# Retention followed by two MLPs: attention from chunk 4 on in half chunks of 64 tokens

## The chip, the cores and the metric

The kernel runs on one core of a Trainium2 chip. The metric is the device time of one execution in microseconds (us); smaller is better. The kernel before takes 568.31 us (median of 3 runs, 567.98 to 568.66).

## The reference

The inputs are q, k and v of shape (2 batches, 8 heads, 768 tokens, 64 features). The result of the attention, laid out as 1536 tokens by 512 features, goes through two MLPs (512 to 2048 to 512).

```python
for t in range(S):                     # retention, per batch and head
    state = gamma * state + outer(k[t], v[t])
    y[t] = scale * (q[t] @ state)
h = x @ w_in                           # first MLP
P = a0 + a1*h + a2*h**2 + a3*h**3
Q = 1 + |b0|*|h| + |b1|*h**2
x = (P / (Q + 1e-6)) @ w_out
h = x @ w_in2                          # second MLP
out = (h * sigmoid(h)) @ w_out2
```

## The kernel before, in words

The attention works in 12 chunks of 128 tokens (`attention(c, ...)`, chunk c is block c // 2 of batch c % 2). Decay factors are folded into v, into the mask and into the output, so that a chunk is plain matmuls. Each chunk has three groups of fp32 matmuls on TensorE:

- **SC** (`sc`, line 503): scores. 8 calls (4 head pairs, 2 heads), each 64 features deep, 128 weight columns, 128 moving columns, into two PSUM banks. VectorE multiplies each bank by the causal mask (`am`, line 510; 128x512, twice a chunk).
- **OUTS** (`outs`): line 545, masked scores times v, 8 calls 128 deep with 64 weight columns and 128 moving columns; and from chunk 2 on line 558, the state times q, 8 calls 64 deep, 64 by 128. For the latter GpSimd copies half of q to the other partition half (`qm`, line 492). VectorE then scales the result (`xf`, two of 128x256), ScalarE rounds it to the high part `xh`, and GpSimd or VectorE takes the low part `xl`.
- **GROW** (`grow`, line 529): k times v for the state, 8 calls 128 deep, 64 by 64; not for chunks 10 and 11. VectorE (ScalarE for chunks 0 and 1) adds the bank to the state `bd`. GROW needs v scaled by the decays (`vn`, line 498, on GpSimd; VectorE for chunk 0).

In the trace each fp32 matmul call is two matmul records, each with its own weight load: 16 records for 8 calls.

The MLPs are matmuls of 128x128 weights by 512 moving columns in three products of split operands: `mm_in` at line 595 (12 a step), `mm_out` at line 672 (3 for each of 4 output banks a step). Weights come by DMA as 64-bit words and are taken apart by ScalarE, VectorE and GpSimd (`weights`, `parted`); `il`, `ol` and `gl` are low parts made on GpSimd in the first part of the kernel. From line 839 on (`joint`) and `remaining` the second MLP follows. The last output bank leaves in two halves (`ends`), the three before it by ScalarE (line 705).

The order of all 2344 operations is written out in a table (`ORDER`, unpacked in `Flow.order`); each engine executes its own operations in that order. Around the change the table of before has, on TensorE: chunk 4's SC, steps 0 and 1 of the first MLP, then in one run OUTS of chunk 4, SC of 5 and 6, GROW of 4, OUTS and GROW of 5, GROW and OUTS of 6. For chunks 7 to 9 SC stands alone between MLP matmuls, and OUTS with GROW behind it stand together; for 10 and 11 SC and OUTS each stand alone. A stretch of attention matmuls with MLP matmuls on both sides is called an island below.

PSUM has eight banks: a0, a1, acc0 to acc3, h0, h1. SC and OUTS of chunk 4 and of chunks 6 to 11 use a0 and a1; the state grows in h0, or acc2 and acc3 for chunks 4 to 6.

Of the kernel before, what the change touches and what calls it, by code (L numbers as in the profile page):

```python
# [11 lines left out]
F32 = mybir.dt.float32  # L12
# [11 lines left out]
R = {"xp": (3,), "vd": (0,), "early": ((0, 7), (2, 8), (3, 9), (4, 12)), "gqd": 0, 'lw': -463.92, 'T0': 689.59, 'tau0': 13.93, 'tau1': 122.19, 'c0': -129.63, 'dc': 67.51, 'conv': 39.61, 'half': 427.29, 'absl': -34.77, 'raw': 455.03, 'ret': 752.06, 'spl': -417.39, 'hi': 301.24, 'lo': 31.56, 'inn': -277.93, 'later': -32.81, 'split': -554.53, 'out': 359.39, 'evac': -363.13, 'qload': -20.08, 'scl': 238.79, 'sc': 858.37, 'am': -44.15, 'gr': 112.48, 'av': -547.62, 'bd': 198.47, 'xh': -201.14, 'xl': 110.32, 'glp': 48, 'lop1': 24, 'lop2': 30, 'scp': 4, 'ps': 17, 'ksc': 103.89, 'qa': -467.29, 'ka': 0, 'late': 20, 'mid': 4, 'pev': -317.29, 'pld': -385.01, 'cg': -489.85, 'wm': 6, 'mk': 26.43, 'ck': 21.3, 'g2': (1, 0, 2), 'ch0': 269.21, 'ch1': -102.81, 'ch2': 64.3, 'ch3': 22.33, 'ch4': -52.46, 'ch5': 5.42, 'ch6': -78.23, 'ch7': 237.84, 'ch8': 90.06, 'ch9': -61.88, 'ch10': -106.39, 'ch11': -212.52, 'ru0': 218.22, 'lu0': -107.8, 'ru1': 40.68, 'lu1': -106.06, 'ru2': 91.09, 'lu2': 146.01, 'ru3': -37.17, 'lu3': -39.51, 'rhalf': 125.38, 'wsum': 20.0, 'kd': 4, 'hb': 20, 'turned': ()}  # L24
# [12 lines left out]
    '|3L%12|4f)Jcf9f9pAzTxCHSr7v{uU@E)GP2iOA%@hK$0eE1GtLNELXpCA$5fZUiLKf@Pz0ex@)Cc{Qp00C3rWw;24eX$_+#zHs<pF??k2FY<KHp',
    '9YL1RLT=D2l~!AVx*Pez*_&;~GqfEieu?$AA@(u`w3Mz1R|4;WsGQ8rNb8tb`S@DVD@Mm;}GaD)<!+#vxc4t70{*j!9AR2W*3-a3q$)VVD}z;Bfp',
    'AYhW4NfIs18T!%HW7UsovSQ|&-blixEaSV>d(YOga<2W3TGjI!jM>BCN*1-cf0Vm=loP}kv39iS#@NaC3?Qt7!$2ph^=i+RvhdZ!4?ZnCWEuO|b*',
    'aeSbSNs~g;ePBxH}N3;iofAJoR16eXY4^esXO+-TUZ+F;%)4Rcd!!<qPy4uhtWb@g#X|R>_@-gJ-m;H@en@1DYzIP;=lMGzQiNgmtNsn6nc%l=y&',  # L40
    'W-Z}A-trtj$uF2QNI3Wv~lIDp>c2V9CDaUgxd;bb&|qL9)b_!;ZtBYcc!&?zd7q^Y=qA{33HQw;ioD=8txq^FpOmSbXCfwAZu0>!2$n1qtjDoRGD',
    'Fgc~55tx!vQEEckg@00J>P^pZ8D^oiw3*`2pGb5J<I*}xLs=;s1$vHKDLdt$EyPrmR$^MpNx3LDrK96`0k=^e`jLuJUfMy$DIX=E^pv0CQwb_SUr',
    '{L<N+oGMRilh_5jRk2dO|<ZF3Ln@s4T^!BJ=}QrwmkxYSL<2L*=MEt;QO(kv7q8tVOk{4(+67RFEoAU8+Y9=o#&%J=B6OVSW0V8c=g;NEPWJwWL>',
    '6nEs_I)QVcux73E((s}%k+EF8FPaWtfJ*QDLhThO<s!A{DGIpe~G>$6MUo@U3&`WwmA7~aep-wcL=F&u(M8DD}dQFpQFMUH@X+ABWIrK9%rS#z!$',
    '`~rq6naYwX%YQKjcGe&4V`H!?W1?}o(|A{>O%8qF+Ha9^fzS))94@_p(WIfj?xS|M29I;C>So#CAvs6=@?z6?BO__APkwqQo2IRDO<QoIl^@MNFj',
    'VC3Rmzd#tk_Ghh>x{<O(%{hLd!PEL@}O^gCU{>v)=8hZ__xBnUU@7D*@^iibksEX5Cr!U_CBx5-11kT^s_ln^x}4Cg3Gh!&EDJ5)44IEgnfceqD2',
    'L$Z)OqzENLiSQ4775<<z6g{+%7$I*c74B25Fd*a!vpHp`9qNQsAz#QJe&yeI9-rdU;VzX4-%8yugUg0;p<XB-+J_3EVwl4*Lx)g5bP69r>hN_K7#',
    'f6*p;%}b=JG+V6e@=T;WWn%T|%5ND8veB0&v&RIgAVAL!&SxbPL~wp`me@$xXs>P8$Y?`P@BJ3$r*~IKoxK#PEIiAq)${!-%ke7xD?N9wvo%e1<d',
    '2uc3MPHjE4tLYp9bh!68e{w<v39$|i{621u}Z9}WDCrl14!h-N~ILbZ4FX0%s3{69?usSpgU--w+I`j@xLc1_E{1oPey`g_t7}kcdVOm%d7KOfHd',
    'gvDxhYevyI2+c5C1GaR7}kfSVN=)_eh*{9=CD7E4(GxjVRkqW{tkV@mM|(T3kSojusm!Hhr+#ZAsi0d!o_et90`AgqhW5i6z+%ZA;QPP<?tX}2@k',  # L50
    '`6;oq<#Tn&%H$`FOGg~wrMh{ij@lW;vm=Q-hNSQT!B<KfTnESw0t!}D-6B;}}lE5zWK9E*2_WSpH}gcSTTB<GZzievN1keYLH9KIdWa2|dY;&Ki?',
    '9nx}MJ{8{coA6Kg#2+{pzYTXnI?m1S!)MMW@i-r!3F$dM-wiqCV~EcsIRk$R3Ag}f<j<iXXX0A?6_?^HQkt_$AuhvTLUt+3wVC-{sKehfat>)Hg}',
    'EFP*X1Hyp6hcxR!+zj_-k&(iMb*-;6xm_H7DUp+>m>58#b=YZ5gBySK)Sy(wH-IZ*I?7xGLw7_R^O-NH%W5eK;$3;1b-Q`|*$L+>r-xSNVoJ@j!0',
    'MMY*H=#5H*kcjitqiq}dt9?aiK7cS1-WGolsAm8&M?#iQ?C9e$OZaj{w^J2~?HFyj!<&8X)yUTd)AwTdE-XatD56&eMxh4P3xn&uj<xM<^H}i7d!',
    'YySouizHEjn8p&ZY5iJB{$>N(p&!G?))>a;-1`7e&GweoqO<~+*!WkUUHsC@@l@s!?}y>;LCiGNAON=BWw5`U*TQ6PTI<D7P-$4_$oi-|M*`X#@A',
    'S7DnH^qJdLmOW8TXyQ+TV~;Po64lj$5q63R`EDo^+p_m!s{O`dTdS;x;gk>r<t5?zu=f7vB5B(WrwWU^k?a!e^82RONGlMNh8Hpo7H!G&Z$|1AUL',
    'C2y1za+~+a-~5+Ukbx3gZpwBkC@Ce56p_M`N)E|gE-DozwcO!K@(&-B%JQ0vNg8>@RVA&w;lol~;>ixFCh6pfRFNa{mP^Pc`9pR}NvSTo<ty1NHR',
    'QJJmAJA@YRY}NB?)Aol#*H!U!KZxDJ}Elnbej#az~!aYxzg&N+wC5^W}x4m*a9&7RY`%CU@nf9FPZ+Q65SLc_rm#p_G-k@~@PWH*!y6>LY0?|49R',
# [77 lines left out]
def retention_two_mlps(  # L136
# [910 lines left out]
```

## Time and profile before

| | |
|---|---|
| time, median of 3 runs | 568.31 us |
| profiled execution: its time / its span | 567.52 us / 565.6 us |
| TensorE busy | 559.9 us (99%) |
| VectorE, ScalarE, GpSimd busy | 435.8, 409.9, 205.8 us |

The span runs from the first to the last instruction of the profile; 1.9 us of the time lie outside it. Matmuls overlap each other, so TensorE's busy share says only that a matmul was under way. How long a group of matmuls holds TensorE is read from the starts in the timeline: an MLP matmul follows the one before it after 0.227 us.

### The profile page before, as it was taken

The page shows a single profiled execution, that of the slowest core. Times are in us where ns is not written, and L with a number is a line of the kernel's source. Part 1 is how long each engine was busy: PE and PEld are TensorE (multiplying, and loading weights), DVE is VectorE, ACT ScalarE, POOL GpSimd, SP SyncE. Part 2 cuts the span into 40 slices and gives each one's busy share as a digit, 9 for nine tenths or more (in the row PEclk, how much of TensorE's full clock was granted, in tenths as well). Part 3 has the DMA queues.
Part 4 walks back from the last instruction along what each step waited for, and adds up shares of the span by engine and source line. Part 5 has one row for each costly group of instructions (what it writes and reads, how often), then busy time and mean ns, then how long its engine had stood idle before and what let it go on. Part 6 is the DMA issues. An engine that isn't in the chain of part 4 may idle for free.

```text
span 565.6 us, 8461 instructions
## 1 busy us (share of the span) xinstructions
PE 559.9 (99%) x2985; PEld 460.6 (81%) x2985; DVE 435.8 (77%) x670; ACT 409.9 (72%) x698; POOL 205.8 (36%) x176
## 2 busy tenths in 40 slices
PE   9999999999999999999999999999999999999997
PEld 7777778888888888888888888888888888888886
DVE  3899899897888797898789687898579889453530
ACT  3789989999898987898899878884445555224432
POOL 4798764574465822624535565200000000000000
PEclk9999999999999999999999999999999999999999
DMA  8999945432233400123144678861413333235602
GB/s 318 322 334 327 331 159 173 150 130 75 74 131 115 146 1 2 62 74 124 40 162 139 226 259 274 283 220 39 148 46 129 120 100 128 75 130 176 198 0 74
DMA packets 42095, 85.05 MB, mean 150 GB/s; under 512 B 4165, under 2 KB 5573, under 8 KB 42054
## 3 DMA queue, kind: packets, MB, share of 16 engines
q1 hardware_dynamic: 41904, 84.43, 44.1%
q8 instruction: 23, 0.38, 0.3%
q14 instruction: 18, 0.15, 0.1%
q10 hardware_dynamic: 150, 0.09, 0.1%
HBM read 63.53 MB, written 20.97 MB: 149 GB/s over the span
## 4 chain that ended last, share of the span: by engine, by line
PE 95%; POOL 2%; DMA 1%; issue 1%; DVE 0%; SPq 0%; ACT 0%; ACTq 0%; POOLq 0%
PE acc L672 46%; PE h L595 19%; PE a L595 11%; PE h L839 7%; PE a L839 7%; PE a L503 2%; PE a L545 1%; POOL il L456 1%; DMA kT<-in_kt_dram 1%; PE a L558 1%; POOL qm L492 1%; PE h L529 0%; PE acc L545 0%; POOL vn L360 0%; POOL xl L360 0%
## 5 line engine op out<-in xcount | busy, mean ns | idle before, releaser
L360 POOL TENSOR_TENSOR gl<-s,gh 128x512 fp32r<-128x512 f32 x48 | 63.3, 1320 | 81.6 <-ACT gh L352 57.7
L672 PE MATMUL acc<-gh,oh 128*128 128x512 f32 x192 | 75.6, 394 | 0.0
L672 PE MATMUL acc<-gh,ol 128*128 128x512 f32 x192 | 74.8, 389 | 0.0
L672 PE MATMUL acc<-gl,oh 128*128 128x512 f32 x192 | 74.7, 389 | 0.0
L672 PE MATMUL acc<-oh,gh 128*128 128x512 f32 x191 | 74.3, 389 | 0.0
L672 PE MATMUL acc<-ol,gh 128*128 128x512 f32 x191 | 74.3, 389 | 0.0
L672 PE MATMUL acc<-oh,gl 128*128 128x512 f32 x191 | 74.3, 389 | 0.0
L595 PE MATMUL h<-xl,ih 128*128 128x512 f32 x168 | 65.5, 390 | 0.4 <-DVE xl L360 0.4
L595 PE MATMUL h<-xh,ih 128*128 128x512 f32 x168 | 65.8, 392 | 0.0
L595 PE MATMUL h<-xh,il 128*128 128x512 f32 x168 | 65.4, 389 | 0.0
L456 POOL TENSOR_TENSOR il<-wt,ih 128x512 fp32r<-128x512 f32 x36 | 49.6, 1384 | 36.8 <-ACT ih L451 32.1
L367 DVE SCALAR_TENSOR_TENSOR wt<-wt,raw 128x512 int32<-128x512 int32 x64 | 55.0, 867 | 8.8 <-ACT wt L352 4.3
L456 POOL TENSOR_TENSOR ol<-wt,oh 128x512 fp32r<-128x512 f32 x36 | 50.8, 1424 | 16.5 <-ACT oh L451 15.1
L352 ACT ACTIVATE raw<-raw,par 128x512 int32<-128x512 uint32 x64 | 48.6, 762 | 1.3 <-DMA raw<-in_moe_w_out_dram 1.2
L367 DVE SCALAR_TENSOR_TENSOR s<-s,par,h 128x512 f32<-128x512 f32 x65 | 48.3, 744 | 1.4
L352 ACT ACTIVATE gh<-s 128x512 fp32r<-128x512 f32 x56 | 35.0, 628 | 12.0 <-PE acc L672 9.2
L352 ACT ACTIVATE wt<-raw 128x512 f32<-128x512 f32 x64 | 42.1, 663 | 1.8 <-DMA raw<-in_moe_w_out_dram 1.7
L672 PEld LDWEIGHTS acc<-gh,oh 128*128 128x128 f32 x192 | 36.0, 188 | 8.1 <-issue 0.2
L672 PEld LDWEIGHTS acc<-gl,oh 128*128 128x128 f32 x192 | 36.0, 188 | 7.5
L672 PEld LDWEIGHTS acc<-oh,gl 128*128 128x128 f32 x191 | 35.9, 188 | 7.5
L672 PEld LDWEIGHTS acc<-gh,ol 128*128 128x128 f32 x192 | 36.1, 188 | 7.2
L672 PEld LDWEIGHTS acc<-oh,gh 128*128 128x128 f32 x191 | 35.8, 188 | 7.4
(287 smaller groups left out, 1319.8 us busy)
## 6 DMA issues: line engine op xcount, KB each, us to landing
raw<-in_moe_w_in_dram SPq DMA_DIRECT2D x32, 512.0 KB, 3.8
raw<-in_moe_w_out_dram SPq DMA_DIRECT2D x32, 512.0 KB, 3.8
spill<-wt SPq DMA_DIRECT2D x48, 256.0 KB, 4.2
wt<-spill SPq DMA_DIRECT2D x48, 256.0 KB, 2.8
qT<-in_qt_dram SPq DMA_DIRECT2D x11, 256.0 KB, 4.8
vn<-in_v_dram SPq DMA_DIRECT2D x11, 256.0 KB, 4.7
kT<-in_kt_dram SPq DMA_DIRECT2D x10, 256.0 KB, 4.6
kn<-in_k_dram SPq DMA_DIRECT2D x9, 256.0 KB, 5.7
```

Of the source, the lines that this page charges most:

```text
L352: lambda: nc.scalar.activation(out=out_, in_=in_, func=func, **kw),
L360: op(eng, dur, rank, lambda: e.tensor_tensor(out=out_, in0=in0, in1=in1, op=alu), reads, writes, port)
L367: lambda: nc.vector.scalar_tensor_tensor(out=out_, in0=in0, scalar=scalar, in1=in1, op0=op0, op1=op1),
L456: e.tensor_tensor(out=at(nm + "l"), in0=from_, in1=at(nm + "h").bitcast(F32), op=ALU.subtract)
L492: nc.gpsimd.tensor_copy(out=out_, in_=in_)
L503: nc.tensor.matmul(heads(sb_[j].t)[:, hp, :], kT_[js, hp, :], qT_[js, hp, :], start=True, stop=True)
L545: nc.tensor.matmul(place(hp, j), vn_[:, 2 * hp + j, :], heads(am[j].t)[:, hp, :], start=(hp % 2 == 0 if more else hp == 0), stop=not more, ...
L558: nc.tensor.matmul(place(hp, j), state.t[rs, 2 * a + j, :], x, start=False, stop=True, skip_group_check=True)
L595: nc.tensor.matmul(h.t, sl.t[w][:, ws], x[g].t[:, c, :], start=(n == 0), stop=(n == 3 * KD - 1))
L672: nc.tensor.matmul(a.t, a1, a2, start=(first and n == 0), stop=((last or apart) and n == 2), skip_group_check=apart)
L839: nc.tensor.matmul(b_.t, w[0](c, wlo), x[0](c, xlo), start=(start and n == 0), stop=(n == 5), skip_group_check=True)
```

## The change

**Chunks 4 to 11 work in halves of 64 tokens** (`halves`; chunks 0 to 3 keep the old form, now called `wholes`). With half 0 and half 1 of a chunk:

- SC computes only the two diagonal 64x64 blocks of each head: 16 calls, 64 deep, 64 weight columns, 64 moving columns. The masks shrink to 128x256 (`near`, made by two GpSimd copies at the start), twice a chunk.
- GROW makes the growth of half 0 and of half 1 in two banks: 16 calls, 64 deep, 64 by 64. VectorE adds them one after the other: state before the chunk, state in the middle (`mid`), state after. Chunks 10 and 11, which had no GROW, get half of one (8 calls), with one add, and load their k.
- OUTS: 8 calls within a half (64 by 64), 16 calls of the two states times q (64 by 64), and 16 calls 32 weight columns wide for the other 8 products within a half. The state of the middle has to be there before OUTS begins.
- Four state buffers take turns. GROW uses acc2 and acc3 for chunks 4 to 6, and for 7 to 11 the banks a0 and a1 that SC and OUTS of the same chunk use.

**Smaller parts.** `ones` and the mask buffers of chunks 0 and 2 lie in MLP buffers; `causal` is made in place; the eviction of output bank 0 in the last group moves from ScalarE to VectorE (`out_on_dve`).

**The order table is new** (2358 operations). On TensorE it has: SC of 4, step 0, GROW of 4, step 1, then in one run OUTS of 4, SC, GROW and OUTS of 5, GROW and SC of 6; then step 2 and two output products, OUTS of 6. For chunks 7 to 11 GROW, SC and OUTS each stand alone: OUTS of 6, step 3, GROW of 7, four output products, SC of 7, two output products, OUTS of 7, step 4, GROW of 8, and so on. On VectorE, `bd` of the middle of chunk 5 comes behind both its masks. On GpSimd `vn` of chunks 4, 6 and 5 comes earlier, ahead of `il` of the second weight pair. Of the start, SC of 3 stands before SC of 1, OUTS of 3 before GROW of 2, and on VectorE one more weight operation (line 432) before chunk 3's `xl`, `bd` of 3 behind it. The table's last 45 operations are the same as before.

```diff
+    def halves(rank, ci, b, grows, sb_, gb_, kT, kT_, qT, qT_, kn, kn_, vn, vn_, qm):
+        side = [slice(n * D, (n + 1) * D) for n in range(2)]
+        was, mid = state_of[b], unused.pop(0)
+        if grows:
+            state_of[b] = unused.pop(0)
+        def grow():
+            for a in range(2):
+                for j in range(2):
+                    for r in range(2):
+                        for t in range(1 + grows):
+                            head = 2 * (2 * r + a) + j
+                            nc.tensor.matmul(
+                                gb_[t].t[side[r], (2 * a + j) * D :][:, 0:D],
+                                kn_[side[t], head, :], vn_[side[t], head, :],
...
+        for t, (from_, to) in enumerate(((was, mid), (mid, state_of[b]))[: 1 + grows]):
...
+            tt("dve", rank + R["bd"], new, sv, old, ALU.add, [gb_[t], from_], [to], n=HP * D, port=False)
+        def sc():
+            for hp in range(HP):
+                for t in range(2):
+                    for j in range(2):
+                        nc.tensor.matmul(
+                            sb_[j].t[side[t], hp * D : (hp + 1) * D],
+                            kT_[side[j], hp, side[t]], qT_[side[j], hp, side[t]],
...
+        def outs():
...
+            turn = ((0, 0), (1, 1), (0, 1), (1, 0))
+            for a in range(2):
+                for r, j in turn:
+                    within(2 * r + a, j, r)
+            for a in range(2):
+                for t, state in enumerate((was, mid)):
+                    for r, j in turn:
+                        x = qT_[side[r], 2 * r + a, side[t]] if r == j else qm.t[side[r], a, side[t]]
+                        mm(2 * r + a, j, t, state.t[side[r], (2 * a + j) * D :][:, 0:D], x)
+            for a in range(2):
+                for n in range(2):
+                    for r, j in turn:
+                        hp, part = 2 - 2 * r + a, slice(j * D + n * D // 2, j * D + (n + 1) * D // 2)
+                        nc.tensor.matmul(
+                            sb_[hp // 2].t[part, a * P + r * D :][:, 0:D],
+                            vn_[side[r], 2 * hp + j, n * D // 2 : (n + 1) * D // 2],
+                            ams[j].t[side[r], hp * D : (hp + 1) * D],
...
+                if g == gb and m == R["out_on_dve"]:
+                    op("dve", 0.6, now + R["evac"],
+                        lambda o=o, a=a: nc.vector.tensor_scalar(out=o.t, in0=a.t, scalar1=0.5, ...
...
+        op("pool", 0.1, -46.0, lambda ns=ns: nc.gpsimd.tensor_copy(out=near.t[ns, :], in_=causal.t[ns, ns]), ...
```

## Rows read from the trace of the kernel before

**Rows 1.** The page: busy time of each engine; shares of the chain that ended last.

```profile
PE 559.9 (99%) x2985; PEld 460.6 (81%) x2985; DVE 435.8 (77%) x670; ACT 409.9 (72%) x698; POOL 205.8 (36%) x176
...
PE 95%; POOL 2%; DMA 1%; issue 1%; DVE 0%; SPq 0%; ACT 0%; ACTq 0%; POOLq 0%
```

**Rows 2.** Busy time by stretch: stretch, length, each engine, PEclk, DMA share, GB/s.

```profile
22.50:30.00 7.50, 7.06 (x45) 5.38 (x48) 6.65 (x10) 6.66 (x12) 6.21 (x7) 1.00 0.90 312
30.00:38.00 8.00, 7.76 (x160) 6.46 (x159) 7.60 (x14) 7.38 (x14) 7.76 (x9) 1.00 1.03 383
38.00:58.00 20.00, 20.00 (x150) 15.88 (x146) 19.16 (x33) 19.11 (x33) 16.92 (x17) 1.00 0.87 299
...
78.00:98.00 20.00, 20.00 (x139) 16.08 (x136) 18.02 (x30) 19.25 (x33) 9.22 (x8) 1.00 0.53 171
```

**Rows 3.** Waits of TensorE: total us, times, longest.

```profile
PE h L595 <- DVE xl L360: 0.4, 1, 0.4
```

**Rows 4.** Timeline of TensorE around SC of chunk 7: start us, us, instructions.

```profile
46.10 0.39 PE L595 MATMUL h<-xh,il 128*128 128x512 f32 x1
46.41 1.16 PE L503 MATMUL a<-qT,kT 64*128 64x128 f32 x16
...
47.84 0.39 PE L672 MATMUL acc<-gh,ol 128*128 128x512 f32 x1
```

**Rows 5.** The same around OUTS and GROW of chunk 7.

```profile
49.46 0.39 PE L672 MATMUL acc<-gl,oh 128*128 128x512 f32 x1
49.77 1.09 PE L545 MATMUL a<-am,vn 128*64 128x128 f32 x16
50.80 0.33 PE L558 MATMUL a<-qT,bd 64*64 64x128 f32 x2
50.81 0.33 PE L558 MATMUL a<-qm,bd 64*64 64x128 f32 x2
50.96 0.28 PE L558 MATMUL a<-qT,bd 64*64 64x128 f32 x2
...
51.07 0.28 PE L558 MATMUL a<-qT,bd 64*64 64x128 f32 x2
...
52.35 0.40 PE L672 MATMUL acc<-gh,ol 128*128 128x512 f32 x1
```

**Rows 6.** Timeline, all engines: the weight loads of GROW of chunk 7.

```profile
51.40 0.55 PEld L529 LDWEIGHTS h<-vn,kn 128*64 128x64 f32 x16 [0.17 <-issue]
```

**Rows 7.** Instructions of line 529: shortest, median, longest in ns; first and last start.

```profile
L529 PEld LDWEIGHTS h<-vn,kn x96: 133/138/138, 12.3 to 78.4; 128*64 128x64 f32 x96
```

**Rows 8.** Timeline of TensorE on either side of OUTS of chunk 11.

```profile
131.31 0.39 PE L672 MATMUL acc<-gl,oh 128*128 128x512 f32 x1
...
133.58 0.39 PE L672 MATMUL acc<-gh,ol 128*128 128x512 f32 x1
```

**Rows 9.** Timeline of TensorE on either side of the run of chunks 4 to 6.

```profile
28.53 0.39 PE L595 MATMUL h<-xh,il 128*128 128x512 f32 x1
...
38.37 0.39 PE L595 MATMUL h<-xl,ih 128*128 128x512 f32 x1
```

**Rows 10.** The chain that ended last, between 20 and 40 us: start us, us, what.

```profile
32.35 1.05 POOL vn L360
```

**Rows 11.** VectorE by form: masks of 128x512, scalings of 128x256; busy us, mean ns.

```profile
L360 DVE TENSOR_TENSOR am<-a,causal 128x512 f32<-128x512 f32 x16 | 10.5, 681 | 0.9 <-PE a L503 0.9
...
L360 DVE TENSOR_TENSOR xf<-a,gq 128x256 f32<-128x256 f32 x16 | 6.2, 416 | 0.6 <-PE a L558 0.4 <-POOL il L456 0.2
```

**Rows 12.** GpSimd by form: copies of 64x256.

```profile
L492 POOL COPY qm<-qT 64x256 f32<-64x256 f32 x18 | 9.6, 536 | 1.3 <-DMA qT<-in_qt_dram 0.3
```

**Rows 13.** Timeline of the end, all engines.

```profile
561.33 0.60 ACT L709 ACTIVATE u<-acc 128x512 f32<-128x512 f32 x1
...
561.72 0.28 PE L644 MATMUL acc<-oh,gl 128*128 128x256 f32 x1
...
562.04 0.66 ACT L647 ACTIVATE s<-acc 128x256 f32<-128x256 f32 x2
```

More of the change, by code (lines that the diff above doesn't have):

```diff
@@ L37 @@
[L37 to L46, printed above, removed]
@@ L323, in temp @@
         return spare[(spared[0] - 1) % len(spare)]
+    ones = ew["u2"].bufs[1]
+    one = ones.t[0:1, 0:P]
     bank = {n: Buf(n, [P, GT], F32, psum) for n in ("a0", "a1", "acc0", "acc1", "acc2", "acc3", "h0", "h1")}
@@ L538, in place @@
-        def place(hp, j):
-            x = xo[hp // 2 % len(xo)]
-            return heads(x.t)[j * D : (j + 1) * D, hp % 2 if len(xo) == 2 else hp, :]
-        def outs():
-            for hp in range(HP):
-                for j in range(2):
-                    nc.tensor.matmul(
-                        place(hp, j),
-                        vn_[:, 2 * hp + j, :],
-                        heads(am[j].t)[:, hp, :],
-                        start=(hp % 2 == 0 if more else hp == 0),
-                        stop=not more,
-                        skip_group_check=True,
-                    )
-            if more:
-                for a in range(2):
-                    for r, j in ((0, 0), (1, 1), (0, 1), (1, 0)):
-                        hp, rs = 2 * r + a, slice(r * D, (r + 1) * D)
-                        x = qT_[rs, hp, :] if r == j else qm.t[rs, a, :]
-                        nc.tensor.matmul(place(hp, j), state.t[rs, 2 * a + j, :], x, start=False, stop=True, skip_group_check=True)
@@ L560, in attention @@
-        if grows:
-            op("pe", 0.6, rank + R["gr"], grow, [kn, vn], [st])
-        op("pe", 1.5 if more else 0.98, rank + R["av"], outs, [vn, *am] + ([state, qT, qm, qm.low] if more else []), xo)
-        if grows:
-            sv, to = st.t[:, 0 : HP * D], state.t[:].rearrange("p a e -> p (a e)")
-            if not more:
-                act(rank + R["bd"], to, sv, AF.Copy, [st], [state], True, n=HP * D)
-            else:
-                tt("dve", rank + R["bd"], to, sv, to, ALU.add, [st], [state], n=HP * D, port=False)
+        if c >= R["near"]:
+            xo = halves(rank, ci, b, grows, sb_, [bank[x] for x in o_banks] or sb_, kT, kT_, qT, qT_, kn, kn_, vn, vn_, qm)
+        else:
+            xo = wholes(rank, c, b, more, sb_, bank[o_banks[0]], sb_ if more else [bank[o_banks[1]]], kT, kT_, qT, qT_, kn, kn_, vn, vn_, qm if more else None)
@@ L904, in spread @@
         for j in range(2):
-            nc.tensor.matmul(bank["acc3"].t[j * D : (j + 1) * D, :], ones.t[:, 0:D], row0[0:1, j * HP * P : (j + 1) * HP * P], start=True, stop=True)
+            nc.tensor.matmul(bank["acc3"].t[j * D : (j + 1) * D, :], one[:, 0:D], row0[0:1, j * HP * P : (j + 1) * HP * P], start=True, stop=True)
     def params():
-        nc.tensor.matmul(bank["acc2"].t[:, 0:6], ones.t, pin.t, start=True, stop=True)
+        nc.tensor.matmul(bank["acc2"].t[:, 0:6], one, pin.t, start=True, stop=True)
     def relate():
```

265 lines of the change are left out of this document (178 added, 87 removed).

## The prediction

> **What bounds the kernel now.** I read the page first: TensorE is busy 99% of the span and carries 95% of the chain that ended last [rows 1]. Busy is not proof, so the waits come next: of TensorE's waits behind the start-up only one is as long as 0.4 us, at 23 us, for a low part on VectorE [rows 3]. From 38 us on it waits for nobody, at granted clock 1.00 in every stretch shown [rows 2]: whatever takes TensorE less time there ends the kernel earlier by as much, as long as the others keep up. Between 22 and 38 us GpSimd is in the chain [rows 10] and busy 13.97 of 15.5 us, with DMA near its limit (0.90 and 1.03) [rows 2]; a gain there is less sure. From 22.5 to 58 us (35.5 us) VectorE is busy 33.41 us and ScalarE 33.15 us [rows 2], so 2 to 2.4 us are free.
>
> **Units for TensorE.** An MLP matmul follows the last after 0.227 us. An island's price is the start of the second MLP matmul behind it less the start of the last one ahead, less 2 x 0.227. For chunk 7: SC 47.84 - 46.10 - 0.45 = 1.29 us [rows 4]; OUTS with GROW 52.35 - 49.46 - 0.45 = 2.44 us [rows 5]; OUTS alone (chunk 11) 133.58 - 131.31 - 0.45 = 1.82 us [rows 8].
> Inside an island, matmuls on different parts of the array start together; I call that a beat. With 128 moving columns a beat lasts 0.11 us (50.96 to 51.07), for fours as for pairs: in the state group four start within 0.02 us [rows 5]. With 64 moving columns the 16 weight loads of GROW take 0.55 us in 8 pairs, each load 0.138: (0.55 - 0.138) / 7 = 0.059 us a beat [rows 6, 7]. So OUTS with GROW has 12 beats of 0.11 and 8 of 0.059, 1.79 us, and 0.65 us are fixed; OUTS alone has 12, 1.32 us, and 0.50 fixed. They differ by one change of tile shape inside: 0.15 us a change, 0.35 us for entering and leaving.
>
> **The islands after.** No row has four 64x64 tiles with 64 moving columns. The bounds of such a beat are 0.059 (as the pair of GROW) and 0.118 (fours don't overlap); I take 0.059, since at 128 columns fours cost what pairs cost [rows 5]. Each call is two records, so:
> - GROW: 16 calls in fours, 8 beats: 0.47 + 0.35 = 0.82 us. Half a GROW (chunks 10, 11) is 8 pairs: also 0.82.
> - SC: 0.82 us.
> - OUTS: 24 calls in fours, 12 beats, 0.71; a change of shape 0.15; 16 calls 32 columns wide; 0.35. These 16 use eight places of the array: 4 beats of eight (0.24) or 8 of four (0.47). I take 4: starts in a four lie 0.007 us apart (0.02 us over three gaps [rows 5]), so eight fit in 0.059. OUTS is 1.45 us, or 1.68.
>
> Chunks 7 to 9: before 1.29 + 2.44 = 3.73, after 0.82 + 0.82 + 1.45 = 3.09: 0.64 us each, **1.92 us** (1.23 with the slower OUTS). Much of the saved streaming goes into a third entry and exit.
> Chunks 10 and 11: before 1.29 + 1.82 = 3.11, after 3.09: 0.02 each, **0.04 us** (-0.42). The added GROW eats the gain.
> Chunks 4 to 6: before, the run from 28.53 to 38.37 costs 9.84 - 0.45 = 9.39 us [rows 9], waits included. After: GROW of 4 alone 0.82; OUTS of 6 alone 1.45; the run 0.35 + OUTS of 4 (1.10 without entry) + 0.15 + SC and GROW of 5 (0.94) + OUTS of 5 (1.10) + 0.15 + GROW and SC of 6 (0.94) = 4.73. Within it OUTS of 5 must wait for one scaling, two masks and the middle state on VectorE, 4 x 0.42 = 1.7 us [rows 11] plus hand-overs of some 0.35, behind OUTS of 4, and SC with GROW and the change of shape cover 1.09: 0.95 us of wait. Together 7.95: **1.4 us** saved (0.7 with the slower OUTS). If GROW of 4 also has to wait for `vn`, which now must come before step 1, up to one `vn`, 1.05 us [rows 10], is lost; I take nothing, as the table puts `il`'s source operations earlier.
>
> **The rest.** VectorE, per chunk: two masks at 0.68 become two at 0.42, and one add of 0.42 comes: -0.10 us [rows 11]; no new load there, but no relief either. GpSimd gets two copies for `near`, at most 0.54 each [rows 12], in the start-up among waits for ScalarE; nothing, and 1.1 us if that cover is gone. The two loads of k (on SP's queue, behind other loads of 78 us and later, where DMA is busy 0.53 [rows 2]) are hidden; if not, chunk 10's GROW waits, bounded by a `vn`-sized delay of 1 us. Start-up: SC of 4 is shorter by 0.47, but step 0 waits for chunk 3's `xl` on VectorE anyway [rows 3], ahead of which one weight operation of about 0.68 has moved and OUTS of 3 is earlier by one GROW; bounds 0.7 either way, taken as nothing. The eviction on VectorE: the halves at the end begin at 562.04, just behind the last matmul (561.72 + 0.28), and ScalarE was free at 561.93 [rows 13]: nothing (0 to 0.1 us loss).
> New waits: in chunks 7 to 11 a0 and a1 go from TensorE to VectorE and back three times a chunk instead of twice (GROW, SC, OUTS). VectorE works in order, and behind each hand-over the next TensorE group of the chunk queues with all MLP matmuls after it. The table has 1.4 to 11 us of MLP matmuls between; the shortest are SC to OUTS of 7 (two products, 1.36 us, against two masks, 0.84, and two weight or MLP operations ahead of them) and GROW to SC of 9. Bounds 0 and some 1.5 us; I take 0.36.
>
> **Sum:** 1.92 + 0.04 + 1.4 - 0.36 = 3.0 us. The profiled 567.52 becomes 564.5; the median of the runs shown lies 0.79 higher, so 568.3 becomes **565.3 us**.
>
> **Rivals.**
> 1. *The 32-wide group takes 8 beats.* For: no row shows eight at once. Against: the 0.007 us between starts [rows 5]. Price 0.23 x 8 = 1.8: 567.1 us.
> 2. *The early stage absorbs its share.* For: GpSimd in the chain, `vn` at 32.35 [rows 10], DMA at its limit [rows 2], and three chunks need GROW before OUTS instead of behind it. Then the 1.4 of chunks 4 to 6 is lost: 566.7 us.
> 3. *Slower: the banks a0 and a1 become the chain.* 5 chunks x 3 hand-overs. If VectorE, busy 19.16 of 20 us [rows 2], is late by one operation of 0.68 at a hand-over, TensorE stands still as long. From five of the fifteen on the gain of 3.4 is gone; with eight, 5.4 - 3.4 = 2.0 us slower: 570.3 us. Against: today SC to OUTS crosses VectorE too, without a wait, and the table leaves mostly over 2 us.
> 4. *The change doesn't do what it says: fours of 64 columns don't overlap.* Beats of 0.118: GROW and SC 1.29, OUTS 20 beats and 0.50, 2.86; a chunk 5.44 instead of 3.73 or 3.11, so 1.71 x 3 + 2.33 x 2 = 9.8 us, and chunks 4 to 6 some 7.0 more than forecast, 5.6 worse than before: 583.7 us. Against: the four within 0.02 us [rows 5].
>    [...]
>
> **Chances.** Forecast 0.58; rival 1 0.15; rival 2 0.12; rival 3 0.11; rival 4 0.04. A measurement can tell about 0.2% (1.14 us) from no change. Faster by more: 0.55 of the forecast, half of rival 1, most of rival 2: 0.71. Within: 0.16. Slower: 0.13. Range: below, no waits at the hand-overs and 0.7 from the start-up and 0.3 elsewhere, 1.4 under the forecast: 563.9. Above, rival 1 with waits of 1 us more: 568.2; beyond it lie rivals 3 and 4.
>
> **What would show it.** Right: around chunk 7 three islands of about 0.82, 0.82 and 1.45 us; in OUTS a beat of 0.059 with four starts in 0.02 us, and eight in the last group; the mask at 0.42; no wait of TensorE longer than 0.3 us behind 38 us; the first matmul of the second MLP earlier by 3 us, and the same end behind it. Wrong: TensorE idle ahead of GROW, SC or OUTS with VectorE as releaser (rival 3), or ahead of GROW of 4 and 5 with GpSimd (rival 2), or islands of 1.7 us and more (rivals 1, 4).

## The result, and the profile after

The changed kernel takes **573.47 us** (median of 5 runs, 571.23 to 574.17); the kernel before, beside it, 568.57 (567.98 to 570.53). The ratio is 1.0076 (95% interval 1.0049 to 1.0104): slower by some 4.9 us, where 565.3 was forecast. The profiled execution took 573.18 us, its span 571.4.

Three marks on TensorE cut the two spans into stages. The marks are the starts of step 0's second MLP matmul, of step 3's last one (chunk 7 begins behind it) and the end of the span. At the second mark the changed kernel still owes six output matmuls of step 0 that the kernel before has done, 6 x 0.227 = 1.36 us.

| | before | after | after, longer by |
|---|---|---|---|
| start to step 0's second matmul | 23.42 | 26.61 | 3.19 |
| from there to step 3's last matmul | 22.68 | 25.15 + 1.36 | 3.83 |
| from there to the end | 519.5 | 519.6 - 1.36 | -1.27 |
| span | 565.6 | 571.4 | 5.8 |

So the stage of chunks 7 to 11 gained and two earlier stages lost. The gain first: TensorE's timeline around chunk 7, GROW, SC and OUTS, as answer to [rows 4, 5].

```profile
51.76 0.39 PE L696 MATMUL h<-xh,il 128*128 128x512 f32 x1
52.08 0.69 PE L557 MATMUL a<-vn,kn 64*64 64x64 f32 x32
...
53.04 0.39 PE L773 MATMUL acc<-gh,ol 128*128 128x512 f32 x1
...
55.34 0.39 PE L773 MATMUL acc<-gl,oh 128*128 128x512 f32 x1
55.65 0.69 PE L575 MATMUL a<-qT,kT 64*64 64x64 f32 x32
...
56.62 0.39 PE L773 MATMUL acc<-gh,ol 128*128 128x512 f32 x1
...
57.55 0.40 PE L773 MATMUL acc<-gl,oh 128*128 128x512 f32 x1
...
58.73 0.45 PE L621 MATMUL a<-am,vn 64*32 64x64 f32 x32
...
59.46 0.40 PE L696 MATMUL h<-xl,ih 128*128 128x512 f32 x1
```

By the forecast's own measure the islands cost 53.04 - 51.76 - 0.45 = 0.83, 56.62 - 55.34 - 0.45 = 0.83 and 59.46 - 57.55 - 0.45 = 1.46 us; forecast were 0.82, 0.82 and 1.45. The 32 records of the 32-wide group take 0.45 us in all and start in four groups of eight (from 58.73, 58.81, 58.87 and 58.92), so they do run eight at a time. The small mask costs 414 ns, as the forecast's 0.42:

```profile
L365 DVE TENSOR_TENSOR am<-a,near 128x256 f32<-128x256 f32 x14 | 5.6, 414 | 0.1
```

The losses are in TensorE's waits (us in total, times, longest), where [rows 3] had 0.4 us at most behind the first microseconds:

```profile
PE a L575 <- issue: 2.6, 1, 2.6
...
PE acc L557 <- POOL vn L365: 0.7, 1, 0.7
PE h L500 <- DVE bd L365: 0.6, 1, 0.6
PE h L696 <- DVE bd L365: 0.6, 1, 0.6
PE h L518 <- DVE s L365: 0.4, 1, 0.4
```

The longest has no releaser: TensorE stops in the middle of SC of chunk 6 with nothing to wait for. TensorE's timeline there:

```profile
38.52 0.34 PE L575 MATMUL a<-qT,kT 64*64 64x64 f32 x7 [0.17 <-DVE xf L365]
41.48 0.57 PE L575 MATMUL a<-qT,kT 64*64 64x64 f32 x23 [2.62 <-issue]
...
42.88 0.63 PE L696 MATMUL h<-xh,ih 128*128 128x512 f32 x1
43.31 0.63 PE L696 MATMUL h<-xl,ih 128*128 128x512 f32 x1
```

Nine of the group's 32 matmul records start by 38.64, the other 23 from 41.48 on. Behind the stop the MLP matmuls of step 2 follow each other after 0.427 us instead of 0.227, until 46.20. The same in busy time by stretch (columns as in [rows 2]):

```profile
33.20:38.60 5.40, 4.35 (x252) 3.62 (x246) 4.64 (x11) 4.59 (x9) 5.28 (x6) 1.00 1.04 401
38.60:41.50 2.90, 0.28 (x10) 0.14 (x11) 2.90 (x6) 2.10 (x4) 2.70 (x4) 1.00 0.66 239
41.50:46.30 4.80, 4.80 (x35) 3.84 (x35) 3.18 (x7) 2.05 (x4) 4.80 (x5) 0.64 0.92 255
46.30:60.00 13.70, 13.70 (x266) 10.45 (x265) 10.20 (x20) 12.53 (x22) 7.90 (x9) 1.00 0.81 289
```

The reader sees three things. Ahead of the stop TensorE takes 498 records in 5.4 us (252 matmuls, 246 weight loads), 92 per us, and the DMA engines are full (1.04). In the stop VectorE, ScalarE and GpSimd go on. Behind it the granted clock is 0.64 on the mean: it fell from 1.00 to 0.50 for 3.4 us (42.66 to 46.08). Eight gaps of 0.2 us more are 1.6 us.

What comes to mind is the instructions themselves. The trace records their transfers (queue q8, kind instruction): 16 KB at a time, one for about 256 records of TensorE, counted from the kernel's start with its matmuls, weight loads and semaphore instructions (28 transfers for 7293 records in the changed kernel, 23 for 6017 before; in the quiet part of the kernel before, transfers begin at 2714, 2971, 3227 and 3481 records). Around the stop:

```text
kernel, place              transfer begins  took  records begun by then  TensorE stands from  goes on at
changed, SC of chunk 6         33.21        1.00          737
                               39.15        0.93         1217                38.64             41.48
                               43.84        2.41         1277
```

Between two transfers TensorE used 480 records, not 256, and stood at record 1217 until 1.40 us behind the end of the next transfer. The second loss is at step 0, the line that answers [rows 3]; its cause is weighed below:

```profile
26.30 0.47 PE L696 MATMUL h<-xh,ih 128*128 128x512 f32 x1 [0.59 <-DVE bd L365]
26.61 0.40 PE L696 MATMUL h<-xl,ih 128*128 128x512 f32 x1
```

### The profile page after: what moved, and what is told of

It is laid out like the page before. It is cut to its first block, busy times and chain, and to the rows that moved or that the text cites. A ratio compares the mean times of both kernels' runs of the same rounds, so it can differ in the third digit from the quotient of the medians.

```text
span 571.4 us, 9763 instructions
## 1 busy us (share of the span) xinstructions
PE 560.5 (98%) x3625; PEld 458.6 (80%) x3625; DVE 432.2 (76%) x679; ACT 408.0 (71%) x697; POOL 206.7 (36%) x178
## 4 chain that ended last, share of the span: by engine, by line
PE 95%; DVE 2%; DMA 1%; issue 1%; POOL 1%; ACT 0%; SPq 0%; ACTq 0%; POOLq 0%; DVEq 0%
PE acc L773 46%; PE h L696 20%; PE a L696 10%; PE h L950 7%; PE a L950 7%; DMA vn<-in_v_dram 1%; PE a L594 1%; PE a L477 1%; PE a L575 1%; PE a L557 1%; PE h L1051 1%; DVE wt L372 0%; PE h L518 0%; PE a L621 0%; POOL vn L365 0%
## 5 line engine op out<-in xcount | busy, mean ns | idle before, releaser
L365 POOL TENSOR_TENSOR gl<-s,gh 128x512 fp32r<-128x512 f32 x48 | 64.8, 1353 | 83.6 <-ACT gh L357 67.4
L696 PE MATMUL h<-xh,ih 128*128 128x512 f32 x168 | 67.5, 402 | 0.6 <-DVE bd L365 0.6
L461 POOL TENSOR_TENSOR ol<-wt,oh 128x512 fp32r<-128x512 f32 x36 | 49.5, 1382 | 23.9 <-ACT oh L456 21.6
```

Source lines behind the costliest of these rows:

```text
L365: op(eng, dur, rank, lambda: e.tensor_tensor(out=out_, in0=in0, in1=in1, op=alu), reads, writes, port)
L461: e.tensor_tensor(out=at(nm + "l"), in0=from_, in1=at(nm + "h").bitcast(F32), op=ALU.subtract)
L696: nc.tensor.matmul(h.t, sl.t[w][:, ws], x[g].t[:, c, :], start=(n == 0), stop=(n == 3 * KD - 1))
```

## The experiments

**Theory:** (a) the run of chunks 4 to 6, 576 small records in a row, uses up TensorE's instructions faster than they come, and the stop takes the clock down; (b) the new order of the start-up costs 3 us; (c) the half chunks themselves gain as forecast. **Rivals:** the stop is a hidden wait on banks or operands; the start-up comes out late whatever the order; the gain is given back somewhere else. "Before" is 568.2 to 568.8 us beside each run.

### Is the stop a lack of instructions?

**Spread.** Only the order changes.

```diff
 TensorE: ... OUTS of 5, GROW of 6,
-  SC of 6, step 2, two products, OUTS of 6
+  step 2, SC of 6, two products, OUTS of 6
 VectorE: both masks of 6 behind the step-1 operation that they would hold up
```

> The changed kernel, with one move on TensorE: step 2's twelve wide matmuls between GROW and SC of chunk 6 (behind SC before), and chunk 6's two masks moved on VectorE behind the step-1 instruction that they would otherwise hold up. No instruction is added or left out. Theory (TensorE runs out of instructions because three chunks of small matmuls use them faster than they are fetched beside a saturated DMA): no stop of TensorE of over 0.6 us without a semaphore between 36 and 44 us, the granted clock stays full from 15 us on, and the time falls by 4 to 4.6 us, to about 569.2. Rival 1 (the stop is a wait that the trace does not show, on chunk 6's banks or its loaded q and k): the stop of 2 to 3 us stands in front of or in SC of chunk 6 again and the time is within 1 us of 573.4. Rival 2 (the stop is real but everything behind it waited for a later thing anyway): the stop goes and the time falls by under 1.5 us.

Measured 571.09 us (569.19 to 573.65), ratio 1.0042 (1.0021 to 1.0062). No wait without a semaphore is left, and the profiled clock stays full; TensorE's waits between 20 and 60 us:

```profile
PE acc L556 <- POOL vn L364: 1.5, 1, 1.5
PE h L695 <- DVE s L371: 1.0, 1, 1.0
```

The stop is gone. Chunk 6's banks had more time here too, so this run alone does not exclude a wait on them; the next one and the places of the stops do. Of the 4.2 us of stop and slow clock only 2.4 us came back, less than the 4 to 4.6 expected: step 2 now stands 1.0 us for bank h0, which step 0's operations on VectorE still read, and GROW of 5 waited 1.5 us for `vn`.

**Extra.** The kernel before, without any half chunk, with 160 extra small matmuls at two places.

```diff
+        def extra(to, w, x):
+            for n in range(160):
+                t, j = slice(n // 2 % 2 * D, ...), slice(n % 2 * D, ...)
+                nc.tensor.matmul(to[n % 2].t[t, 0:D], w[j, t], x[j, t], start=True, stop=True)
...
+            if c == 5:
+                extra(sb_, kT_[:, 0, :], qT_[:, 0, :])     # ahead of SC of 5
...                                                         # a like loop ahead of step 36
```

> The kernel before with 160 extra small matmuls (64 rows, 64 columns, their results overwritten) at two places: ahead of SC of chunk 5 (near 30 us, where the DMA engines are 0.87 to 0.94 busy) and ahead of step 36's matmuls (near 220 us, DMA share 0.00). No half chunk is in it. At the changed kernel's rate (16 such in 0.47 us) each set takes 4.7 us. Theory (small matmuls use up the fetched instructions, and the next ones come late where the DMA is full): TensorE stops inside or right behind the first set, without a semaphore, for 1.5 us or more, and does not in the second (under 0.5 us). Rival 1 (instructions are fetched too slowly whatever the DMA does): a stop of about the same length in both. Rival 2 (the stop in the changed kernel has to do with its banks or operands, not with the number of instructions): no stop in either. Time 578.5 us without stops, 580 to 583 with the first.

Measured 585.83 us (2 runs, 585.1 and 586.57). Stops in both places, of different length (timeline; then busy time by stretch):

```profile
36.95 3.38 PE L502 MATMUL acc<-qT,kT 64*64 64x64 f32 x128 [3.75 <-issue]
...
41.77 0.81 PE L502 MATMUL acc<-qT,kT 64*64 64x64 f32 x39 [1.45 <-issue]
...
251.99 1.03 PE L601 MATMUL h<-xh,ih 64*64 64x64 f32 x53 [1.88 <-issue]
```

```profile
33.00:37.00 4.00, 0.25 (x17) 0.11 (x9) 0.00 (x0) 2.83 (x6) 4.00 (x4) 0.93 1.01 380
...
245.00:249.00 4.00, 4.00 (x211) 3.57 (x213) 2.67 (x5) 2.66 (x5) 2.65 (x2) 1.00 0.02 4
```

```text
kernel, place              transfer begins  took  records begun by then  TensorE stands from  goes on at
extra, near 30 us              22.18        1.00          526
                               34.70        0.94          961                32.98             36.95
                               39.51        0.94         1157                40.11             41.77
extra, near 246 us            245.23        1.35         3751
                              249.13        1.44         4188               249.89            251.99
```

A lack of instructions it is: small matmuls alone make the stop, in a kernel without half chunks, and TensorE goes on 1.3 to 1.4 us behind the end of a transfer each time. My theory said "not in the second place", and that was wrong: with the DMA engines idle (0.02) two transfers still begin 3.9 us apart, while 256 records of this kind last 1.9 us (64 in 0.47). With full DMA engines it is worse, 5.2 us of stops instead of 1.9.

The places of the stops say the same. In the 18 traces of this case TensorE's waits show the releaser "issue" 12 times between 12 and 570 us, and each time TensorE stands at record 961, 1217 or 4289: 1217 in the changed kernel, all three here, 961 or 1217 or both in six of the runs below. What comes next differs (SC, GROW, the extra matmuls, a wide one), but the numbers lie multiples of 256 apart, and about 256 records are what goes with one transfer of 16 KB. A hidden wait on banks or operands would have no reason to keep to them.

**Less DMA.** The changed kernel with ten transfers cut to an eighth: two loads, four spills, and the four loads that bring the spills back.

```diff
+                few = P // 8 if (u == 1 and half) or (l, p) == (0, 0) else P
...
-                    dma(..., dst, src..., ...)            # loads of pair 1's output weights
+                    dma(..., dst[0 : few if u == 1 else P], src...[0 : few if u == 1 else P], ...)
...
-                        dma(..., kept.t, wt.t, ...)       # spills of pair 0
+                        dma(..., kept.t[0 : few if u == 0 else P], wt.t[0 : few if u == 0 else P], ...)
```

> The changed kernel, same instructions in the same order, but eight of its transfers carry an eighth of their rows: step pair 1's two output-weight loads (512 KB each) and pair 0's four spills and their way back (256 KB each). This leaves out part of the computation: those weights are not whole. Some 1.6 MB of the 5.6 MB that move between 28 and 44 us are gone, 4 us at 400 GB/s. Theory (the instruction block stands behind a full DMA): the stop in SC of chunk 6 falls from 2.6 us to under 1 us and the clock drop behind it goes; 573.4 becomes 569 to 570. Rival (only the number of instructions per us counts): the stop stays over 2 us and the time within 1 us of 573.4.

Measured 569.16 us (568.36 to 571.34).

```profile
36.03 0.28 PE L558 MATMUL acc<-vn,kn 64*64 64x64 f32 x3 [0.20 <-issue]
...
40.15 0.57 PE L576 MATMUL a<-qT,kT 64*64 64x64 f32 x23 [1.07 <-issue]
```

```profile
33.20:38.60 5.40, 4.31 (x229) 3.44 (x218) 4.15 (x10) 4.83 (x9) 5.28 (x6) 1.00 0.76 242
...
41.50:46.30 4.80, 4.80 (x97) 3.75 (x95) 4.58 (x10) 4.77 (x9) 4.71 (x5) 1.00 0.97 294
```

With the DMA share ahead of it down from 1.04 to 0.76 the same instructions in the same order stop for 1.3 us instead of 2.6 (under 1 expected), and the clock stays at 1.00. The time falls by 4.3 us; up to 1.2 of it may be plain relief from bytes, by the control further down.

Where the time goes can be read from the transfers. From the start of record 961 to that of record 1217 the changed kernel takes 5.64 us: 3.31 until the next instruction transfer begins, 0.93 for it, and 1.40 until TensorE goes on. With less DMA it is 1.89 + 0.88 + 1.36 = 4.13 us, and between records 4033 and 4289 of extra, with the DMA engines idle ahead of it (0.02), 1.15 + 1.44 + 1.42 = 4.0 us. Small records use up 256 in 1.9 us, so even the quickest of these leaves a stop, and beside data the transfer begins later. That it waits in a queue behind the data is argued from this, not seen.

### What did the start-up cost?

**Start-up as before.**

```diff
 all engines and SP: operations ahead of step 0's first matmul
-  in the new table's order
+  in the old table's order
```

> The changed kernel, with only the order of the work ahead of step 0's first matmul put back to that of the kernel before, on every engine and on SP. Theory (two separate losses, one of them the new order of the start-up): step 0's second matmul comes near 23.4 us of the span again instead of 26.6, and the time falls by about 3.1 us, to about 570.3; TensorE still stops in the SC of chunk 6 without a semaphore (2 to 3 us), since nothing there is changed. Rival (the start is late because of the 64-wide masks and state additions themselves, not because of the order): step 0 stays near 26 us and the time near 573.4.

**The reverse:** the kernel before with the new table's order of the same operations.

> The kernel before, whole chunks everywhere, with the changed kernel's order of the work ahead of step 0. Theory 1 (the start-up order costs 3 us by itself, and putting it back in the changed kernel gave 1.0 only because three half chunks behind it ran out of instructions and loads instead): step 0's second matmul near 26.5 us and 571 to 571.6 us. Theory 2 (the start-up's delay is made good before 50 us in any kernel, since weights and loads set that stage): step 0's second matmul near 26.5 us, but the time within 1 us of 568.5.

Step 0's second matmul came at 23.00 us in the first and at 25.37 in the second, which shows it so:

```profile
25.37 0.39 PE L594 MATMUL h<-xl,ih 128*128 128x512 f32 x1
```

The times are 572.4 us for the first (expected 570.3) and 571.58 for the second (expected 571 to 571.6; ratio 1.0050, 1.0032 to 1.0068). In the second, step 0 is 1.1 us earlier than expected, and GROW behind it waits 1.1 us for `vn`. With the new order that matmul came between 24.95 and 27.04 us in five executions of five kernels, with the old between 22.77 and 23.91 in thirteen. So the order is the cause, and by itself it costs 3.4 us. But in the changed kernel putting it back returns 1.0: step 3's last matmul starts at 51.78, as in the changed kernel (51.76), because GROW of 4 and 5 now wait 2.3 us for `kn` and `vn`, the stop is there again (2.5 us, at record 1217 again), and in and behind it the granted clock is 0.50 for 6.8 us (39.53 to 46.36), twice as long as in the changed kernel.

**Both edits.**

> Both edits together: the start-up order of the kernel before, and step 2's matmuls between GROW and SC of chunk 6. Theory: the two losses are separate and add: 573.4 - 3.1 - 4.3 = about 566.0, faster than the kernel before (568.4). Rival (one loss hides the other, as both push the same weights or the same clock): 568 to 570.

Measured 568.95 us, ratio 1.0006 (0.9986 to 1.0025). Together they give 4.5 us, more than 1.0 + 2.4, since the earlier start counts once the stop is gone. But 3 us are missing against 566.0; the time is the rival's (568 to 570). TensorE's waits between 20 and 60 us:

```profile
PE acc L556 <- POOL vn L364: 1.9, 2, 1.7
PE h L695 <- DVE xl L364: 1.2, 1, 1.2
PE h L695 <- ACT wt L356: 1.0, 1, 1.0
PE h L695 <- issue: 0.5, 1, 0.5
```

### Where is the rest of the gain?

**Chunk 5's v first** (the kernel above, v of 5 loaded and scaled ahead of v of 6).

> All half chunks from chunk 4, both order edits of the earlier run (start-up order of the kernel before, step 2's matmuls ahead of SC of chunk 6), and chunk 5's v loaded and scaled ahead of chunk 6's. In the run without that last edit GROW of chunk 5 waited 1.7 us for the scaled v. Theory (waits for loads in chunks 4 to 6 are what holds the half chunks back there): that wait falls under 0.4 us and the time from 568.95 to about 567.2. Rival (the transfers come no faster: the next load is late instead): within 0.6 us of 568.95.

Measured 570.39 us, neither the theory's 567.2 nor within 0.6 us of 568.95. The wait for `vn` fell from 1.9 to 0.2 us, and others took its place, the lack of instructions (at record 961) first among them:

```profile
PE acc L556 <- issue: 1.6, 1, 1.6
PE h L695 <- DVE xl L364: 1.1, 1, 1.1
```

**Halves from chunk 7 on only.** Chunks 4 to 6 whole, with the old table up to step 3. Four versions, each mending in the table the wait that the last one showed: `vn` of chunk 7 (2.9 us); its two state additions ahead of a weight operation; its two masks ahead of a step-2 operation.

```diff
-R = {..., "near": 4, ...}
+R = {..., "near": 7, ...}
```

> Half chunks only from chunk 7 on: chunks 4 to 6 whole as in the kernel before, and the order of the kernel before up to step 3; from there the changed kernel. Theory (what the halves give in chunks 7 to 9 is real, 1.92 us, and neither loss belongs to them): 568.4 - 1.9 = 566.5, no stop without a semaphore over 0.6 us before 60 us. Rival (halves beside the wide matmuls gain nothing, for instance because wide matmuls behind them are later by what the islands are shorter): 568.4.

> Half chunks from chunk 7 on as in the run before of that kind, but chunk 7's v and k are loaded, and its v is scaled on Pool, earlier: there TensorE waited 2.9 us for that scaling, which came from the order table, not from the half chunks. Theory (the halves of chunks 7 to 11 are worth about 1.9 us once nothing waits): 570.4 - 2.9 = 567.5 at most, 566.5 by the kernel before less 1.9; no wait of TensorE over 0.7 us behind 25 us. Rival (another late operand takes the place of that one): 568.5 to 570.

> The last kernel with half chunks from chunk 7 on, with one more move: chunk 7's two state additions on VectorE ahead of a weight conversion, so that the two score banks are free when SC of chunk 7 comes (it waited 0.36 + 1.3 us there). Theory (the matmul gain of chunks 7 to 11 is real: from the last matmul of step 3 to the end the changed kernel's trace takes 1.28 us less than that of before, once its six later matmuls of step 0 are taken off): 568.5 - 1.3 = 567.2, no wait of TensorE over 0.3 us behind 25 us; the time from step 3's last matmul to the end of the span, 519.5 in the trace of before, is 518.2 to 518.4. Rival (a late operand again): that time is over 519 us.

> Half chunks from chunk 7 on, start-up and chunks 4 to 6 as before the change, and one last move: chunk 7's two masks on VectorE ahead of the step-2 instruction that waits for ScalarE. In the run before of this kind OUTS of chunk 7 waited for them, 1.4 us in all (0.9 ahead of its first matmul, the rest inside). Theory (what is left of the change is a real gain of 1.3 us in chunks 7 to 11): no wait of TensorE over 0.3 us behind 25 us, 518.2 to 518.4 us from step 3's last matmul to the end of the span (519.5 in the kernel before), and a time 1.0 to 1.6 us under that of the kernel before beside it: 566.6 to 567.2. Rival (the next late operand takes it): over 519 us, and a time within 0.5 us of the kernel before.

Measured 570.41, 568.19, 568.02 and 568.81 us; the ratios are 1.0027, 0.9999, 0.9989 (0.9971 to 1.0006) and 0.9995 (0.998 to 1.001). The first is slower than theory and rival said. In the other three the rival won, "another late operand": in the third version OUTS of 7 waited 0.8 us at its entry for masks, and in the last, with that mended, step 4 waited for weights (TensorE's waits, 25 to 100 us):

```profile
PE h L705 <- ACT raw L365: 0.9, 1, 0.9
PE a L603 <- DVE am L373: 0.5, 1, 0.5
```

**Exit on ScalarE** (the third of these, with the last group's bank 0 evicted by ScalarE as before).

> The same with the last output tile's exit back on ScalarE, as before the change. Theory (the exit on VectorE delays the output's issues on SP: in the changed kernel's trace the span ends 4.12 us behind the start of the last matmul, in that of before 3.92): 3.92 again, and 0.2 us less than the run beside it, 567.0. Rival (the 0.2 is chance or is hidden): 4.12 again.

Measured 569.61 us: not decided. The span ends 4.04 us behind the last matmul's start, between 3.92 and 4.12; the time rose through early waits (`vn` twice, 0.7 and 0.3) that have nothing to do with the exit.

**Few bytes.** 20 early transfers, and the 12 later ones that bring the spills back, cut to an eighth, in four kernels: the kernel before, both edits, halves from 7 on, the changed kernel.

```diff
+                few = P // 8 if l == 0 and p < 3 else P    # spills of pairs 0 to 2, and back
+                some = P // 8 if u in (1, 2) else P        # loads of pairs 1 and 2
```

> The kernel before, with 20 transfers cut to an eighth of their rows: the loads of weight pairs 1 and 2 (eight of 512 KB) and the spills of pairs 0 to 2 (twelve of 256 KB) and their way back. Those weights are not whole, so part of the computation is left out; every instruction and its order stand. It is the control for the other three. Both theories: the kernel before waits for loads hardly at all behind 22 us (0.8 us in its trace), so 568.0, within 0.7 us of 568.4.

> Half chunks from chunk 4 on with the two order edits (start-up as before, step 2's matmuls ahead of SC of chunk 6), and the same 20 transfers cut. With whole transfers this order took 568.95 us, and TensorE waited 1.9 us for scaled v, 1.2 us for xl, 1.0 us for weights and 0.5 us without a semaphore. Theory 1 (what the forecast promised in chunks 4 to 6 is lost to transfers that come late): those waits fall by 2 us or more, and the time is 2.0 to 3.0 us under the control: 565 to 566. Theory 2 (the engines that prepare weights and masks set that stage, not the transfers): the waits move to VectorE, ScalarE and Pool, and the time is within 1 us of the control.

> Half chunks from chunk 7 on (the last of those kernels) with the same 20 transfers cut. With whole transfers TensorE waited 0.9 us for ScalarE's weight conversion ahead of step 4 and 0.5 us for a mask. Theory 1: these go, 518.2 to 518.5 us from step 3's last matmul to the end, 1.0 to 1.5 us under the control. Theory 2: they stay or move; within 0.6 us of the control.

> The changed kernel as it is, with the same 20 transfers cut. What is left by theory 1 is the start-up (3.1 us late), a stop for instructions that is 1 us instead of 2.6 with no clock drop, and the gain of 2.0 to 2.7: control + 1.4 to 2.2, near 570. Theory 2: control + 3 or more.

| with few bytes | time, us | against the control |
|---|---|---|
| before (control) | 567.27 (566.82 to 567.89) | |
| both edits | 567.77 (566.62 to 570.83) | +0.5 |
| halves from 7 on | 566.76 (566.51 to 567.79) | -0.5 |
| changed kernel | 568.43 (566.31 to 570.99) | +1.2 |

The control itself is 1.2 us faster than with whole transfers (ratio 0.9979, 0.9970 to 0.9988), more than expected. With both edits the waits for `vn` are gone and the stop is 0.4 us, yet the time is the control's; what is left between 20 and 60 us is VectorE's:

```profile
PE h L697 <- DVE xl L364: 1.4, 1, 1.4
PE h L697 <- DVE s L371: 1.0, 1, 1.0
PE acc L558 <- issue: 0.4, 1, 0.4
```

In that profile the clock fell too, behind the first of these waits: it is 0.95 on the mean from 15 to 25 us and 0.83 from 25 to 32, 3.4 us at 0.50. In the third kernel the 0.9 us for ScalarE's weight conversion stays although the bytes are gone. So theory 2 holds for these two: transfers hold `vn` and lengthen the stop, but behind them stand VectorE and ScalarE. The changed kernel comes out nearer theory 1 (+1.4 to +2.2 expected). Its two stops are 1.0 and 0.8 us, the clock stays full, and step 0's second matmul is 2.2 us later than in the control (24.95 against 22.78); what the halves give stands against these, and +1.2 is the sum, which no run takes apart.

## Why the prediction was wrong, step by step

- **Units and islands: right.** 0.83, 0.83, 1.46 us for 0.82, 0.82, 1.45; the 32 records of the 32-wide group, on different parts of the array, start within 0.24 us (58.73 to 58.97); chunks 7 to 9 gain 0.62 each, 1.86 instead of 1.92. Rivals 1 and 4 fall.
- **Hand-overs of a0 and a1: 0.36 forecast, none seen.** No wait of TensorE over 0.3 us stands behind 46 us. Rival 3, the slower case that I gave most to, is not what happened; the kernel is slower for reasons that no rival named.
- **Chunks 7 to 11 in all: 1.96 less 0.36 forecast, 1.27 measured.** The islands gave 1.8; against them stand 0.20 at the end ("0 to 0.1" in the forecast; below), 0.15 at one change from output products to a step near 197 us, and 0.2 over 2167 gaps of 226.9 instead of 226.8 ns.
  The end, as answer to [rows 13] (start us, us):

```profile
566.88 0.69 DVE L811 TENSOR_SCALAR u<-acc 128x512 f32<-128x512 f32 x1 [6.35 <-PE acc L773]
...
567.27 0.28 PE L745 MATMUL acc<-oh,gl 128*128 128x256 f32 x1
567.59 0.66 ACT L748 ACTIVATE s<-acc 128x256 f32<-128x256 f32 x2 [0.79 <-PE acc L745]
567.60 0.33 SPq L830 DMA_DIRECT2D out_dram<-u  x1
568.03 0.92 SPq L749 DMA_DIRECT2D out_dram<-s  x2
```

  The eviction takes 0.69 us on VectorE, where ScalarE took 0.60. Its issue on SP then ends at 567.93, beside the first half's end (567.98), and the span ends 4.12 us behind the last matmul's start, not 3.92. That the eviction causes these 0.2 us is not shown: with the exit on ScalarE again it was 4.04.
- **Start-up: "taken as nothing, bounds 0.7 either way". This step failed.** It cost 3.2 us, by the order (3.4 in the kernel before with that order). I weighed the pieces I saw moved, SC of 4, one weight operation, OUTS of 3, at their durations. What they set off was larger: OUTS of chunk 0 comes ahead of any other SC and waits for its mask (0.4 us); the trace's first record of the granted clock, at 1.00, begins at 15.36 us instead of 12.20; SC of 3 and 1, ahead of it, take 3.7 us together (11.29 to 15.01, a pair of records every 0.21 us), where SC of 3 and 2, behind it in the kernel before, took 2.0 (12.94 to 14.92, a pair every 0.11); GROW of 3 waits 0.6 us for the state's addition in h0, and step 0 stands 0.6 us for the addition of chunk 3's state, which has moved behind `xl` and holds bank h0. No run takes these pieces apart.
- **Chunks 4 to 6: 1.4 us forecast. This step failed by what it left out.** The step priced matmuls and semaphores and had no term for how fast instructions come. The half form has more than twice the records (288 a chunk instead of 128, matmuls and weight loads), and the table puts 576 of them in a row where the DMA engines are full [rows 2]. The starts around the three islands (GROW of 4, the run, OUTS of 6):

```profile
28.92 0.39 PE L696 MATMUL h<-xh,il 128*128 128x512 f32 x1
...
30.20 0.39 PE L696 MATMUL h<-xl,ih 128*128 128x512 f32 x1
...
32.49 0.39 PE L696 MATMUL h<-xh,il 128*128 128x512 f32 x1
...
42.32 0.39 PE L696 MATMUL h<-xl,ih 128*128 128x512 f32 x1
...
47.57 0.39 PE L773 MATMUL acc<-gl,oh 128*128 128x512 f32 x1
...
49.47 0.39 PE L696 MATMUL h<-xl,ih 128*128 128x512 f32 x1
```

  By the forecast's measure they cost 0.83 + 9.38 + 1.45 = 11.66 us, where 7.95 was forecast and 9.39 stood before. Of the 3.7 us above the forecast the stop is 2.8, counted from start to start. The wait for `vn` is 0.9, at GROW of 5; the forecast weighed one at GROW of 4 and took nothing. VectorE holds the run up by 0.7, where 0.95 was forecast, and 0.3 is left over. So the matmuls themselves were priced about right (5.1 us in the run for 4.73). The slow clock behind the stop, which had no term either, adds 1.6; with the 2.3 us by which the islands cost more than before, that is the 3.83 of the table, within 0.1.
- **Rival 2 (the early stage absorbs its share) was right as to what comes next.** With the stop and the start-up mended the chunks wait for `vn`, then for `xl`, for step 0's operations in h0, and for weights; no version with whole transfers can be told from the kernel before as faster. Its 566.7 us is not reached either, since the gain of chunks 7 to 9 is partly absorbed in the same way: chunk 7's masks and step 4's weights are late as soon as TensorE is early.

Open: what holds an instruction transfer's beginning back beside data, and whether a longer search for an order would let the early stage keep the 1.3 us of chunks 7 to 11.

## What to carry to other kernels

Cutting a matmul into more and smaller ones multiplies instructions: before placing a row of them, count records against the supply that the trace shows (here, in the bursts, one transfer of 16 KB began 3.9 us behind the last with the DMA engines idle in between (0.02, extra), and 5.9 us behind it beside full ones (1.04, changed kernel; 4.8 in extra, where they were full up to 37 us)), and keep wide matmuls between them (with step 2's there, spread had no stop). A wait with the releaser "issue" in the middle of one group, behind a burst of small instructions, was the sign here; places a multiple of 256 records apart (961, 1217, 4289) confirmed it. When a new order table comes with a change, price its start-up as a change of its own, and look in the trace for the second latest operand at each place where TensorE is to become earlier.

## What the runs showed of the hardware that was not expected

- TensorE can run out of instructions: a stop of 1.9 us behind a burst with the DMA engines idle (0.02, extra), and stops of 2.6 us (changed kernel, 1.04) and 3.75 us (extra, 1.01) behind bursts with full ones. It stood at records 961, 1217 and 4289 alone, multiples of 256 apart, and went on 1.3 to 1.4 us behind the end of the 16 KB transfer.
- A stop can cost much of its length again by the clock: 1.6 us behind 2.6 in the changed kernel. In or behind stops of 2.6 us (the changed kernel) and 3.75 us (extra) the granted clock was 0.50 for 3.4 us, and in and behind one of 2.5 us (start-up as before) for 6.8 us; behind 1.3 us (less DMA) and 1.9 us (extra, second place) it stayed at 1.00. The length alone does not decide: a wait of 1.4 us for VectorE (both edits, few bytes) was followed by 3.4 us at 0.50.
- Eight 64x32 matmul records start within 0.05 us (58.73 to 58.78 in the changed kernel), and the next eight 0.06 to 0.08 us behind the first.
